# Strassen factors of the last layer's weights: made in every cell, or made once and streamed from HBM

## The chip, the cores and the metric

The kernel runs on one core of one Trainium2 chip. The metric is device time of one execution in microseconds (us). Three executions of the kernel before took 1265.14, 1265.29 and 1268.28 us; the median is 1265.29.

Engines are named as in the profile: PE is TensorE's matmul, PEld its weight load, DVE is VectorE, ACT is ScalarE, POOL is GpSimd, SP is SyncE, which issues all DMAs here.

## The reference, cut to what matters

Three stages follow each other: attention with 32 packed queries (8 batches, 8 heads, 576 tokens, width 64), an expert layer with softmax gating and layer norm (512 to 1024 to 512), and a maxout layer ("moe2", 512 to 768 to 512), on 4608 tokens. The change touches the last stage, and the decoding of its weights:

```
def _moe2_ref(x, w1, w2, w3, w_out):
    h = np.maximum(np.maximum(x @ w1, x @ w2), x @ w3)
    return (h @ w_out).astype(np.float32)
```

The weights arrive as 64-bit floats. The kernel reads them as pairs of 32-bit words and turns them into 32-bit floats itself ("decoding").

## The kernel before, in words

**Precision.** PE multiplies in a reduced 32-bit format. Every operand is split into a high part (an ACT copy into that format) and a low part (the value minus the high part), and a product is three matmuls: high x high, high x low, low x high.

**First half (to about 549 us).** A loop over 36 tiles of 128 tokens does attention for one batch after another (class Packed), the hidden layer (tok_hidden, L494), the transposes (L559) and the output product y (L574), which goes to a DRAM tensor, ydram. Letters in CFG['s1'] say in which order these steps are issued. At each letter D the pieces loaded at the D before are decoded and up to CFG['dr'] new ones loaded: 128 rows by 256 columns each, one ACT step, five DVE steps (L127 to L136), one POOL step (L141). The decoded moe2 weights go to the DRAM tensors wdram and wodram. Only the first EARLY x 128 = 512 of the 768 columns of w1, w2, w3, and the first 512 of the 768 rows of w_out, are done here.

**Second half.** x is cut into six passes (p) of 768 tokens, each a 2x2 block of 384-token columns and halves of the 512 inputs. The 768 hidden units are three column pairs (c) of 2 x 128, and there are three weight matrices (x, printed as w1 to w3). One "cell" (p, c, x), 54 in all, computes a 2x2 block product of one weight block and the x block by Strassen's scheme in Winograd's form: seven products instead of eight, each 2 row blocks x 3 matmuls of 384 columns, 42 matmuls per cell (L701). The four PSUM banks ba, bb, bc and bd hold products; a later product is added into a bank that has been used (start=False) after the bank's first content was read:

```
product(bc, 's3', 't3'); v_ = bc + u      (DVE, L734)
product(bd, 's1', 't1'); result(1, 1, bd, v_)
product(ba, 'a12', 'b21', start=False)
product(bc, 'a22', 't4', start=False)     (must wait until v_ was read from bc)
```

The token factors (b11, t1 to t4, b21, b22) are made once per pass: load_y (L654), four differences on DVE (sums_y, L660), seven splits on ACT with DVE and POOL in turn (splits_y, L674). The weight factors are made anew **for every cell**, one cell ahead, by split_w (L634): four sums s1 to s4 on DVE (L638 to L641, tile s, one buffer), three high parts on ACT (L647), three low parts on POOL (L648: al of 512, sl of 1024, cl of 256 columns; two buffers each). All raw weights stay in SBUF. The columns beyond 512 are decoded in the first pass (decode_late, L605).

After the first cell of a pass, after its fourth and at its end come output blocks: per 128 hidden units out_step (L914) does 9 matmuls of 512 columns (L918), after split_hidden (L747) made the high and low part of h (ACT L750, POOL L751). store (L923) scales on ACT and writes out. Per pass these are 108 matmuls (54 in the first pass and 54 more at the very end).

**Order.** The program is traced in this order, and a scheduler of the language gives each engine a fixed sequence at compile time, by readiness in its own model, earlier traced first. On the chip each engine runs its sequence in order; a waiting instruction holds all behind it. SP's DMAs are such a sequence too.

Of the kernel before, what the change touches and what calls it, by code (L numbers as in the profile page):

```python
# [18 lines left out]
def f32(ap):  # L19
# [17 lines left out]
    dr=2,  # L37
# [7 lines left out]
    early=4,  # L45
    wr=3,
    l3='v',
    mx3='v',
# [7 lines left out]
    d3='g',  # L56
# [6 lines left out]
def kernel(  # L63
# [20 lines left out]
    EARLY = CFG['early']  # L84
# [18 lines left out]
    wodram = tc.dram_tile([DF2, DM], F32, name="wodram")  # L103
    ydram = tc.dram_tile([P, KDM, NT], F32, name="ydram")
# [494 lines left out]
    wr = [[None] * 3 for _ in range(KF2)]  # L599
    w2h = [None] * KF2  # L600
    w2l = [None] * KF2
    raw_b, split_b, split_a = {}, {}, {}
    B_ORDER = ('b11', 't2', 't3', 't1', 'b21', 't4', 'b22')

    def decode_late(dst, src):  # L605
        raw = raw_p.tile([P, KDM, P, 2], I32, tag="raw", name="raw")
        nc.sync.dma_start(out=raw, in_=src)
        t = raw_p.tile([P, DM], F32, tag="dt", name="dt")
        decode(dst, raw.rearrange("r k f t -> r (k f) t"), t, None, ENG[CFG['mx3']], ENG[CFG['d3']])()

    def load_w2(c, x, pool):
        wr[c][x] = pool.tile([P, KDM, P], F32, name=f"wr{c}_{x}")
        if c < EARLY:
            nc.sync.dma_start(
                out=wr[c][x], in_=wdram[x, :, c * P:(c + 1) * P].rearrange("(k r) f -> r k f", r=P)
            )
        else:
            decode_late(
                wr[c][x].rearrange("r k f -> r (k f)"),
                words((w1, w2, w3)[x])[:, c * P:(c + 1) * P, :].rearrange("(k r) f t -> r k f t", r=P),  # L620
            )

    def load_wo2(c, pool):
        wt = wst.tile([P, DM], F32, tag="wt", name="wt3")
        if c < EARLY:
            nc.sync.dma_start(out=wt, in_=wodram[c * P:(c + 1) * P, :])
        else:
            decode_late(wt, words(w_out2)[c * P:(c + 1) * P, :, :].rearrange("r (k f) t -> r k f t", f=P))
# [5 lines left out]
    def split_w(c, x):  # L634

        a, a2 = wr[2 * c][x], wr[2 * c + 1][x]
        s = st_p.tile([P, 4, 2, P], F32, tag="s", name="s")
        nc.vector.tensor_tensor(out=s[:, 0], in0=a2[:, :2, :], in1=a2[:, 2:, :], op=ALU.add)  # L638
        nc.vector.tensor_tensor(out=s[:, 1], in0=s[:, 0], in1=a[:, :2, :], op=ALU.subtract)
        nc.vector.tensor_tensor(out=s[:, 2], in0=a[:, :2, :], in1=a2[:, :2, :], op=ALU.subtract)  # L640
        nc.vector.tensor_tensor(out=s[:, 3], in0=a[:, 2:, :], in1=s[:, 1], op=ALU.subtract)  # L641
        ah, al = (sw_p.tile([P, 2, 2, P], F32R, tag=n, name=n) for n in ("ah", "al"))
        ch, cl = (sw_p.tile([P, 2, P], F32R, tag=n, name=n) for n in ("ch", "cl"))
        sh, sl = (sw_p.tile([P, 4, 2, P], F32R, tag=n, name=n) for n in ("sh", "sl"))
        av = a.rearrange("r (h k) f -> r h k f", h=2)
        for hi, lo, src in ((ah, al, av), (sh, sl, s), (ch, cl, a2[:, 2:, :])):
            nc.scalar.copy(hi, src)  # L647
            nc.gpsimd.tensor_tensor(out=lo, in0=src, in1=f32(hi), op=ALU.subtract)  # L648
        split_a[c, x] = dict(
            a11=(ah[:, 0], al[:, 0]), a12=(ah[:, 1], al[:, 1]), a22=(ch, cl),  # L650
            **{f's{i + 1}': (sh[:, i], sl[:, i]) for i in range(4)},
        )

    def load_y(p):  # L654
        for key, k, n in (('b11', 0, 0), ('b12', 0, 1), ('b22', 1, 1), ('b21', 1, 0)):
            t = raw_b[p, key] = yb_p.tile([P, 2, TW], F32, tag=key, name=key)
# [3 lines left out]
    def sums_y(p):  # L660

        def step(key, x, y, dst=None):
            def do():
                t = raw_b[p, dst] if dst else yb_p.tile([P, 2, TW], F32, tag=key, name=key)
                nc.vector.tensor_tensor(out=t, in0=raw_b[p, x], in1=raw_b[p, y], op=ALU.subtract)
                raw_b[p, key] = t
# [21 lines left out]
    def cell(p, c, x):  # L688


        fa = split_a.pop((c, x))
# [39 lines left out]
        add(out=u, in0=bb, in1=q, op=ALU.add)  # L731
        product(bc, 's3', 't3')
        v_ = row("v")
        add(out=v_, in0=bc, in1=u, op=ALU.add)  # L734
        product(bd, 's1', 't1')
        result(1, 1, bd, v_)
        product(ba, 'a12', 'b21', start=False)
        if x == 0:
            nc.scalar.copy(cur[0, 0], ba)
        else:  # L740
            add(out=cur[0, 0], in0=ba, in1=cur[0, 0], op=ALU.max)
        product(bc, 'a22', 't4', start=False)
        result(1, 0, bc, u)
        product(bd, 's4', 'b22', start=False)
        result(0, 1, bd, u)

# [136 lines left out]
    yb_p = ctx.enter_context(tc.tile_pool(name="yb", bufs=1, **right))  # L883
    w0_p = ctx.enter_context(tc.tile_pool(name="w0", bufs=1, **right))
    st_p = ctx.enter_context(tc.tile_pool(name="st", bufs=1, **right))
    sw_p = ctx.enter_context(tc.tile_pool(name="sw", bufs=2, **right))
    sy_p = ctx.enter_context(tc.tile_pool(name="sy", bufs=1, **right))
    load_y(0)
    for x in range(3):
        for c in range(2):  # L890
            load_w2(c, x, w0_p)
    before = [*sums_y(0), *splits_y(0), lambda: split_w(0, 0)]
    j = NB - 1
    for _ in range(2 * KFF):
        step_y(j, 2 * KFF)
        step_t(j, done[j] + CFG['look'])
        if before:
            before.pop(0)()
    late.close()


    wpool = ctx.enter_context(tc.tile_pool(name="w2", bufs=1, reuse_waits="tile"))
    wst = ctx.enter_context(tc.tile_pool(name="wst", bufs=1, reuse_waits="tile"))
    raw_p = ctx.enter_context(tc.tile_pool(name="raw", bufs=1, reuse_waits="tile"))
    z_p = ctx.enter_context(tc.tile_pool(name="scales", bufs=1, reuse_waits="tile"))
    cur_p = ctx.enter_context(tc.tile_pool(name="cur", bufs=2, reuse_waits="tile"))
    keep_p = ctx.enter_context(tc.tile_pool(name="kept", bufs=8, reuse_waits="tile"))
    tmp_p = ctx.enter_context(tc.tile_pool(name="tmp", bufs=2, reuse_waits="tile"))
    h_p = ctx.enter_context(tc.tile_pool(name="h2", bufs=3, reuse_waits="tile"))
    o_p = ctx.enter_context(tc.tile_pool(name="o", bufs=3, reuse_waits="tile"))  # L910
# [22 lines left out]
    todo = [lambda c=c: load_wo2(c, wpool) for c in range(2)]  # L933
    for x in range(3):
        todo += [lambda c=c, x=x: load_w2(c, x, wpool) for c in (2, 3)]
    for x in range(3):
        todo += [lambda c=c, x=x: load_w2(c, x, wpool) for c in (4, 5)]
    todo += [lambda c=c: load_wo2(c, wpool) for c in range(2, KF2)]
    cells = [(p, c, x) for p in range(NT // TW // 2) for c in range(KF2 // 2) for x in range(3)]
    z = scales()  # L940
    kept, first_half, ops = [], [], None
    for n, (p, c, x) in enumerate(cells):
        for _ in range(3):
            if todo:
                todo.pop(0)()
        if n + 1 < len(cells):
# [63 lines left out]
```

## Time and profile before

| | before |
|---|---|
| median of three runs | 1265.29 us |
| profiled execution | 1260.86 us |
| its span, first to last instruction | 1258.8 us |
| mean granted TensorE clock | 0.946 of full speed |
| busy: PE, PEld, DVE, ACT, POOL | 89%, 73%, 70%, 42%, 40% |
| HBM read, written | 63.97 MB, 23.07 MB |

The profile is one execution, taken by the hardware profiler. A group row reads: line, engine, operation, tile written <- tiles read, shape, count | busy us, mean ns of one | idle time of the engine just before, and what ended it. "L648" is a line of the kernel. Matmul ends are modelled: two consecutive ones overlap in the record, so their rate is read from their starts.

### The profile page before, as it was taken

The numbers are of one execution on the slowest core, as the hardware profiler recorded it, in microseconds if no ns is written. First come the engines' busy times: TensorE is split into PE (matmuls) and PEld (weight loads), VectorE is DVE, ScalarE is ACT, GpSimd is POOL, SyncE is SP. The second block draws the span as 40 slices with busy tenths as digits, with TensorE's granted clock in tenths as the row PEclk, the third lists the DMA queues.
The fourth block names the chain that finished last, engine by engine and source line by source line (L and its number), as shares of the span: only waits on it lengthen the run. The fifth ranks groups of instructions, "written<-read, shape, count | busy, mean of one in ns | idle before, by whom it ended". The sixth has DMA issues, their size and how long they took to land.

```text
span 1258.8 us, 17413 instructions
## 1 busy us (share of the span) xinstructions
PE 1115.5 (89%) x6308; PEld 918.6 (73%) x6308; DVE 884.8 (70%) x1668; ACT 528.2 (42%) x1025; POOL 505.4 (40%) x385
## 2 busy tenths in 40 slices
PE   4789899999999999798778998888888879879888
PEld 3357576777677778577666887788878868878887
DVE  6798777787878776779899558555845584564561
ACT  4476464655555544523243323322422333233222
POOL 5442210111111100247467546455734564465552
PEclk8799999999999999898998998898899889989999
DMA  8734344444444400533112001100200020001001
GB/s 235 171 90 117 102 115 128 121 132 115 137 116 125 111 18 17 161 97 94 51 42 68 26 1 38 39 25 1 76 26 1 1 76 26 1 1 51 1 1 50
DMA packets 96550, 88.16 MB, mean 70 GB/s; under 512 B 47569, under 2 KB 79313, under 8 KB 96465
## 3 DMA queue, kind: packets, MB, share of 16 engines
q1 hardware_dynamic: 96464, 87.06, 24.3%
q8 instruction: 49, 0.80, 0.3%
q14 instruction: 37, 0.30, 0.1%
HBM read 63.97 MB, written 23.07 MB: 69 GB/s over the span
## 4 chain that ended last, share of the span: by engine, by line
PE 51%; DVE 16%; issue 8%; POOL 7%; ACT 4%; DMA 3%; ACTq 0%; POOLq 0%; DVEq 0%
PE m L701 21%; PE o L918 10%; PE y L582 8%; PE h L507 5%; POOL sl L648 4%; PE tp L564 2%; PE mp L402 1%; DVE u L731 1%; DVE v L734 1%; DVE s L640 1%; DMA wdram<-dt 1%; DVE raw L131 1%; POOL hl L751 1%; DVE r L723 1%; DVE dt L127 1%
## 5 line engine op out<-in xcount | busy, mean ns | idle before, releaser
L648 POOL TENSOR_TENSOR sl<-s,sh 128x1024 fp32r<-128x1024 f32 x54 | 135.6, 2511 | 51.1 <-ACT sh L647 46.6
L638 DVE TENSOR_TENSOR s<-wr 128x256 f32<-128x256 f32 x54 | 50.1, 927 | 116.1 <-POOL sl L648 115.1
L648 POOL TENSOR_TENSOR al<-wr,ah 128x512 fp32r<-128x512 f32 x54 | 76.7, 1421 | 133.6 <-ACT ah L647 133.5
L582 PE MATMUL y<-lh,woh 128*128 128x512 f32 x288 | 119.4, 417 | 0.7 <-DVE yt L250 0.6
L582 PE MATMUL y<-ll,woh 128*128 128x512 f32 x288 | 115.3, 401 | 1.6 <-DVE ll L571 1.6
L582 PE MATMUL y<-lh,wol 128*128 128x512 f32 x288 | 115.0, 399 | 1.1 <-POOL wol L219 1.1
L141 POOL TENSOR_TENSOR dt<-raw,dt 128x256 f32<-128x256 f32 x40 | 32.7, 817 | 205.1 <-DVE dt L136 105.3
L701 PE MATMUL m<-t4h,ch 128*128 128x384 f32 x108 | 45.4, 420 | 75.5 <-DVE v L734 75.5
L647 ACT CAST ah<-wr 128x512 fp32r<-128x512 f32 x54 | 33.5, 620 | 147.9 <-PE m L701 141.6
L918 PE MATMUL o<-w2l,hh 128*128 128x512 f32 x216 | 87.7, 406 | 5.4 <-POOL w2l L632 5.4
L918 PE MATMUL o<-w2h,hh 128*128 128x512 f32 x216 | 88.0, 407 | 0.0
L701 PEld LDWEIGHTS m<-t4h,ch 128*128 128x128 f32 x108 | 23.2, 215 | 88.0 <-DVE v L734 88.0
L918 PE MATMUL o<-w2h,hl 128*128 128x512 f32 x216 | 87.1, 403 | 0.0
L647 ACT CAST sh<-s 128x1024 fp32r<-128x1024 f32 x54 | 56.7, 1050 | 49.8 <-PE m L701 24.0
L648 POOL TENSOR_TENSOR cl<-wr,ch 128x256 fp32r<-128x256 f32 x54 | 51.1, 946 | 54.9 <-ACT ch L647 54.9
L731 DVE TENSOR_TENSOR u<-m,q 128x384 f32<-128x384 f32 x54 | 29.7, 550 | 53.7 <-PE m L701 52.6
L582 PEld LDWEIGHTS y<-lh,woh 128*128 128x128 f32 x288 | 54.5, 190 | 15.3 <-DVE yt L250 1.0
L582 PEld LDWEIGHTS y<-lh,wol 128*128 128x128 f32 x288 | 54.6, 190 | 14.2 <-POOL wol L219 1.6
L570 ACT ACTIVATE lh<-tp,g_sb 128x512 fp32r<-128x512 f32 x72 | 47.3, 686 | 41.2 <-PE tp L564 41.2
L582 PEld LDWEIGHTS y<-ll,woh 128*128 128x128 f32 x288 | 54.7, 190 | 12.9 <-DVE ll L571 2.3
L724 DVE TENSOR_TENSOR kept<-r,kept 128x384 f32<-128x384 f32 x72 | 58.1, 807 | 1.8
L513 DVE TENSOR_REDUCE nm<-h 128x1 f32<-128x1024 f32 x36 | 43.9, 1218 | 20.2 <-PE h L507 19.9
(196 smaller groups left out, 3386.6 us busy)
## 6 DMA issues: line engine op xcount, KB each, us to landing
kt<-in_k_dram SPq DMA_DIRECT2D x16, 576.0 KB, 5.0
vt<-in_v_dram SPq DMA_DIRECT2D x16, 576.0 KB, 5.0
ydram<-yt SPq DMA_DIRECT2D x36, 256.0 KB, 3.2
b<-ydram SPq DMA_DIRECT2D x24, 384.0 KB, 3.4
out_dram<-ob SPq DMA_DIRECT2D x36, 256.0 KB, 2.0
qtl<-in_q_dram SPq DMA_DIRECT2D x64, 128.0 KB, 3.2
raw<-in_moe_w_dram SPq DMA_DIRECT2D x24, 256.0 KB, 2.8
raw<-in_moe_w_in_dram SPq DMA_DIRECT2D x8, 512.0 KB, 8.5
```

The costliest lines, as they stand in the source:

```text
L141: add.tensor_tensor(out=dst, in0=f32(hi), in1=t, op=ALU.add)
L507: nc.tensor.matmul(h[:, n, :], lhsT=x, rhs=m[:, g, n * 512:(n + 1) * 512], start=(i == 0), stop=(i == len(ops) - 1),)
L513: nc.vector.tensor_reduce(out=nm, in_=hv, axis=AX.X, op=ALU.max, negate=True)
L570: nc.scalar.activation(lh, tp, AF.Copy, scale=gc)
L582: nc.tensor.matmul(ys[half][m], lhsT=w[:, kc, ms], rhs=x, start=(kc == 0 and i == 0), stop=(kc == KFF - 1 and i == 2),)
L638: nc.vector.tensor_tensor(out=s[:, 0], in0=a2[:, :2, :], in1=a2[:, 2:, :], op=ALU.add)
L647: nc.scalar.copy(hi, src)
L648: nc.gpsimd.tensor_tensor(out=lo, in0=src, in1=f32(hi), op=ALU.subtract)
L701: nc.tensor.matmul(out, lhsT=w, rhs=y, start=start and i == 0, stop=i == len(ops) - 1, skip_group_check=not start,)
L724: add(out=cur[m, n], in0=r, in1=cur[m, n], op=ALU.max)
L731: add(out=u, in0=bb, in1=q, op=ALU.add)
L918: nc.tensor.matmul(ops[i], lhsT=x[:, ts], rhs=w, start=(c == 0 and n == 0), stop=(c == KF2 - 1 and n == 2),)
```

## The change

Weight factors are made once, in the first pass, for each of the nine weight blocks (c, x). a11, a12 and a22 (high and low) stay in SBUF. s1 to s4 (high and low together, 256 KB each) are written to a DRAM tensor, sdram, and from the second pass on are read back, four tiles per cell, through a ring of nine buffers, issued at the start of the cell before. In the first pass the split of the next cell is cut into steps, and cell() calls one step after each of its products; so are load_wo2 and, in the last cell of a pass, the token splits, which were issued after the cell. The differences and the load of the next pass's tokens move to later cells of the pass. All moe2 weights are decoded in the first half: 56 pieces of 256 columns instead of 40, three per turn instead of two; decode_late is gone. The buffers of h and of the output go from three to two each, and several pools change sides.

```
-    dr=2,
+    dr=3,
-    early=4,
+    sdram = tc.dram_tile([DF2 // 2 // P * 3, 4, P, 4 * P], F32, name="sdram")
+    def split_w(c, x, pool):
+        raw = []
+        def load():
+            for m in range(2):
+                t = w_p.tile([P, 2, 2, P], F32, tag="w", name="wt2")
...
+                nc.sync.dma_start(out=..., in_=wdram[x, :, cs].rearrange("(k r) f -> r k f", r=P))
+        def part(hi, lo, src):
+            nc.scalar.copy(hi, src)
+            nc.gpsimd.tensor_tensor(out=lo, in0=src, in1=f32(hi), op=ALU.subtract)
+        def plus(key, x, y, op):
+            t = sums_w[key] = w_p.tile([P, 2, P], F32, tag=key, name=key, bufs=1)
+            nc.vector.tensor_tensor(out=t, in0=x, in1=y, op=op)
+        def piece(key):
+            t = sr_p.tile([P, 2, 2, P], F32R, tag="s", name=key)
+            part(t[:, 0], t[:, 1], sums_w[key])
+            nc.sync.dma_start(out=sdram[3 * c + x, S_ORDER.index(key)], in_=...)
+            split_s[c, x, key] = t
+        def first():    # ah, al kept in SBUF; sums s1, s2
+        def second():   # piece s2; sum s3
+        def third():    # piece s3; sum s4
+        def fourth():   # piece s1
+        def fifth():    # ch, cl kept in SBUF; piece s4
+        return [load, first, second, third, fourth, fifth]
+    def load_s(c, x):
+        for i, key in enumerate(S_ORDER):
+            t = split_s[c, x, key] = sr_p.tile([P, 2, 2, P], F32R, tag="s", name=key)
+            nc.sync.dma_start(out=f32(t).rearrange("r n k f -> r (n k f)"), in_=sdram[3 * c + x, i])
...
-    def cell(p, c, x):
+    def cell(c, x, between):
+        def others():
+            if between:
+                between.pop(0)()
         product(ba, 'a11', 'b11')
         q = row("q")
         nc.scalar.copy(q, ba)
+        others()
         product(bb, 's2', 't2')
...
+    sr_p = ctx.enter_context(tc.tile_pool(name="sr", bufs=9, **right))
+    w_p = ctx.enter_context(tc.tile_pool(name="w", bufs=3, **right))
-    h_p = ctx.enter_context(tc.tile_pool(name="h2", bufs=3, reuse_waits="tile"))
-    o_p = ctx.enter_context(tc.tile_pool(name="o", bufs=3, reuse_waits="tile"))
+    h_p = ctx.enter_context(tc.tile_pool(name="h2", bufs=2, reuse_waits="tile"))
+    o_p = ctx.enter_context(tc.tile_pool(name="o", bufs=2, reuse_waits="tile"))
+    for n in range(NC - 1):
+        chores[n] = prep[n][1:]
+        if n + 1 < len(prep):
+            chores[n].append(prep[n + 1][0])
+        if n < KF2:
+            chores[n].append(lambda c=n: load_wo2(c, wpool))
+    for p in range(1, NP2):
+        chores.setdefault(NC * p - 7, []).append(lambda p=p: load_y(p))
+        for i, f in enumerate((0, 1, 2, 3)):
+            chores.setdefault(NC * p - 5 + i, []).append(lambda p=p, i=i: fresh(p)[i]())
+        chores.setdefault(NC * p - 1, []).extend([lambda: None] + splits_y(p))
     for n, (p, c, x) in enumerate(cells):
-        if n + 1 < len(cells):
-            split_w(*cells[n + 1][1:])
+        if p and n + 1 < len(cells) or n == NC - 1:
+            load_s(*cells[n + 1][1:])
-        cell(p, c, x)
+        cell(c, x, chores.pop(n, []))
```

## Rows read from the trace of the kernel before

**Rows 1.** The page, part 1: busy us (share of the span) xinstructions.
```profile
PE 1115.5 (89%) x6308; PEld 918.6 (73%) x6308; DVE 884.8 (70%) x1668; ACT 528.2 (42%) x1025; POOL 505.4 (40%) x385
```

**Rows 2.** Stretches of the first half: length, busy (x) by engine, clock, DMA share, GB/s.
```profile
210.00:240.00 30.00, 29.84 (x170) 21.17 (x167) 28.23 (x64) 16.79 (x37) 5.76 (x7) 1.00 0.32 89
300.00:330.00 30.00, 29.77 (x209) 23.35 (x209) 21.52 (x54) 17.33 (x41) 3.27 (x5) 1.00 0.57 159
```

**Rows 3.** Stretches: the first pass, and the five later ones.
```profile
548.80:680.30 131.50, 104.77 (x481) 91.47 (x481) 116.06 (x175) 42.33 (x73) 78.15 (x52) 0.92 0.23 69
680.30:1258.80 578.50, 507.12 (x2485) 465.16 (x2483) 340.61 (x549) 188.39 (x316) 306.18 (x206) 0.94 0.07 25
```

**Rows 4.** The same stretches, PE and PEld of one line: L701, L918, L582.
```profile
680.30:1258.80 578.50, 367.87 (x1890) 350.51 (x1889) 0.94 0.07 25
...
680.30:1258.80 578.50, 144.42 (x595) 114.83 (x594) 0.94 0.07 25
...
548.80:680.30 131.50, 11.94 (x49) 8.84 (x48) 0.92 0.23 69
```

**Rows 5.** One undisturbed cell (L701) and one output block (L918).
```profile
1192.40:1199.70 7.30, 7.29 (x42) 7.29 (x42) 1.00 0.01 2
...
1149.10:1161.70 12.60, 12.57 (x54) 9.97 (x54) 1.00 0.00 0
```

**Rows 6.** Waits from 690 us on: us in total, times, longest.
```profile
DVE s L638 <- POOL sl L648: 107.5, 41, 3.7
...
PE m L701 <- DVE v L734: 65.5, 29, 5.4
```

**Rows 7.** Timeline of DVE in a stalled cell: start, us, instruction [idle before].
```profile
1182.52 1.20 DVE L638 TENSOR_TENSOR s<-wr 128x256 f32<-128x256 f32 x1 [2.99 <-POOL sl L648]
1183.65 0.55 DVE L731 TENSOR_TENSOR u<-m,q 128x384 f32<-128x384 f32 x1
...
1185.39 0.55 DVE L734 TENSOR_TENSOR v<-m,u 128x384 f32<-128x384 f32 x1
```

**Rows 8.** Timeline of PE in a twin of that cell, two passes earlier.
```profile
958.64 0.46 PE L701 MATMUL m<-t4h,ch 128*128 128x384 f32 x1 [3.25 <-DVE v L734]
...
959.86 0.52 PE L701 MATMUL m<-t4l,ch 128*128 128x384 f32 x1
960.18 0.52 PE L701 MATMUL m<-t4h,cl 128*128 128x384 f32 x1
```

**Rows 9.** Stretch just behind that wait.
```profile
959.50:961.00 1.50, 1.50 (x6) 1.50 (x6) 0.26 (x1) 0.40 (x1) 0.05 (x1) 0.50 0.04 11
```

**Rows 10.** Groups by line, whole span.
```profile
L648 POOL TENSOR_TENSOR sl<-s,sh 128x1024 fp32r<-128x1024 f32 x54 | 135.6, 2511 | 51.1 <-ACT sh L647 46.6 <-PE m L701 2.7 <-DMA raw<-in_moe_w_dram 1.6
...
L648 POOL TENSOR_TENSOR al<-wr,ah 128x512 fp32r<-128x512 f32 x54 | 76.7, 1421 | 133.6 <-ACT ah L647 133.5
...
L648 POOL TENSOR_TENSOR cl<-wr,ch 128x256 fp32r<-128x256 f32 x54 | 51.1, 946 | 54.9 <-ACT ch L647 54.9
...
L751 POOL TENSOR_TENSOR hl<-kept,hh 128x384 fp32r<-128x384 f32 x36 | 39.3, 1099 | 15.2 <-ACT hh L750 15.2
...
L750 ACT CAST hh<-kept 128x384 fp32r<-128x384 f32 x36 | 18.3, 512 | 34.1 <-PE o L918 34.1
```

**Rows 11.** Groups of DVE by line, 161.6 to 424.8 us.
```profile
L131 DVE SCALAR_TENSOR_TENSOR raw<-raw,dt 128x256 int32<-128x256 int32 x31 | 14.3, 460 | 0.6
```

**Rows 12.** DMA issues: count, KB each, median us from issue to landing.
```profile
wr<-wdram SPq DMA_DIRECT2D x12, 256.0 KB, 4.8
...
wt<-wodram SPq DMA_DIRECT2D x4, 256.0 KB, 3.2
```

**Rows 13.** Instructions of line L724: ns min/median/max, first and last start.
```profile
L724 DVE TENSOR_TENSOR kept<-r,kept x72: 542/560/2209, 578.5 to 1234.7; 128x384 f32<-128x384 f32 x72
```

**Rows 14.** Timeline of PE in the hand-over.
```profile
529.92 1.11 PE L564 MATMUL tp<-ident,u 128*128 128x128 f32 x4 [6.84 <-DVE u L531]
```

**Rows 15.** Stretch of the hand-over between the halves.
```profile
516.20:531.00 14.80, 7.96 (x40) 6.21 (x38) 12.74 (x16) 8.30 (x12) 5.26 (x3) 0.81 0.88 273
```

More of the change, by code (lines that the diff above doesn't have):

```diff
@@ L590, in y_product @@
                 nc.sync.dma_start(out=ydram[:, half * KDM // 2 + m, j * TB:(j + 1) * TB], in_=yt)
-    wr = [[None] * 3 for _ in range(KF2)]
+    NC = KF2 // 2 * 3
     w2h = [None] * KF2
     w2l = [None] * KF2
-    raw_b, split_b, split_a = {}, {}, {}
+    raw_b, split_b, split_a, split_s = {}, {}, {}, {}
     B_ORDER = ('b11', 't2', 't3', 't1', 'b21', 't4', 'b22')
[L605 to L621, printed above, removed]
-    def load_wo2(c, pool):
[L624 to L628, printed above, removed]
+    S_ORDER = ('s2', 's3', 's1', 's4')
+    def load_wo2(c, pool):
+        wt = w_p.tile([P, DM], F32, tag="w", name="wt3")
+        nc.sync.dma_start(out=wt, in_=wodram[c * P:(c + 1) * P, :])
         w2h[c] = pool.tile([P, DM], F32R, name=f"w2h{c}")
@@ L632, in load_wo2 @@
         nc.gpsimd.tensor_tensor(out=w2l[c], in0=wt, in1=f32(w2h[c]), op=ALU.subtract)
[L634 to L646, printed above, removed]
+    def split_w(c, x, pool):
[3 more added lines that the diff above has]
+                t = w_p.tile([P, 2, 2, P], F32, tag="w", name="wt2")
+                cs = slice((2 * c + m) * P, (2 * c + m + 1) * P)
+                nc.sync.dma_start(
+                    out=t.rearrange("r h k f -> r (h k) f"),
+                    in_=wdram[x, :, cs].rearrange("(k r) f -> r k f", r=P),
+                )
+                raw.append(t)
+        def part(hi, lo, src):
@@ new lines, in piece @@
+        def piece(key):
+            t = sr_p.tile([P, 2, 2, P], F32R, tag="s", name=key)
+            part(t[:, 0], t[:, 1], sums_w[key])
+            nc.sync.dma_start(out=sdram[3 * c + x, S_ORDER.index(key)], in_=f32(t).rearrange("r n k f -> r (n k f)"))
+            split_s[c, x, key] = t
+        def first():
+            ah, al = (pool.tile([P, 2, 2, P], F32R, name=f"{n}{c}_{x}") for n in ("ah", "al"))
+            part(ah, al, raw[0])
+            split_a[c, x] = dict(a11=(ah[:, 0], al[:, 0]), a12=(ah[:, 1], al[:, 1]))
+            plus('s1', raw[1][:, 0], raw[1][:, 1], ALU.add)
+            plus('s2', sums_w['s1'], raw[0][:, 0], ALU.subtract)
@@ new lines, in second @@
+        def second():
+            piece('s2')
+            plus('s3', raw[0][:, 0], raw[1][:, 0], ALU.subtract)
+        def third():
+            piece('s3')
+            plus('s4', raw[0][:, 1], sums_w['s2'], ALU.subtract)
+        def fourth():
+            piece('s1')
+        def fifth():
+            ch, cl = (pool.tile([P, 2, P], F32R, name=f"{n}{c}_{x}") for n in ("ch", "cl"))
+            part(ch, cl, raw[1][:, 1])
+            split_a[c, x]['a22'] = ch, cl
+            piece('s4')
+        return [load, first, second, third, fourth, fifth]
@@ L734, in cell @@
         add(out=v_, in0=bc, in1=u, op=ALU.add)
+        others()
         product(bd, 's1', 't1')
         result(1, 1, bd, v_)
+        others()
         product(ba, 'a12', 'b21', start=False)
@@ L931, in banks_o, with fresh @@
         return [ps_o.tile([P, DM], F32, tag="o", name="o") for _ in range(TW // P)]
[L933 to L939, printed above, removed]
+    NP2 = NT // TW // 2
+    cells = [(p, c, x) for p in range(NP2) for c in range(KF2 // 2) for x in range(3)]
+    chores = {}
+    prep = [split_w(*cells[n][1:], wpool if cells[n][1] else w0_p) for n in range(1, NC)]
+    prep[0][0]()
+    for n in range(NC - 1):
[9 more added lines that the diff above has]
+        chores.setdefault(NC * p - 1, []).extend([lambda: None] + splits_y(p))
+    sums_of = {}
+    def fresh(p):
+        if p not in sums_of:
+            sums_of[p] = sums_y(p)
+        return sums_of[p]
     z = scales()
```

60 lines of the change are left out of this document (24 added, 36 removed).

## The prediction

> **What bounds the kernel now.** I read the page first, then stretches, then waits. The page's totals give TensorE (PE) 89% busy [rows 1], but that is a mean over two halves. The stretches split it. In the attention and first-expert half, PE is within 1% of always busy even where VectorE (DVE) is at 28.2 of 30 us [rows 2]: PE bounds it. The second half is 54 cells of 42 matmuls: nine cells per pass, six passes. The first pass, from the first cell's first matmul, takes 131.5 us, the other five 578.5 us together [rows 3]; the matmuls by line are counted in [rows 4]. What would PE alone need? A cell that never waits shows it: 42 matmuls in 7.29 us, 0.1736 us each; an undisturbed output block of 54 takes 12.57 us, 0.2328 each [rows 5].
>
> Later passes: 1890 x 0.1736 + 594 x 0.2328 = 328.1 + 138.3 = 466.4 us, so 112 of the 578.5 are lost. First pass: 378 x 0.1736 + 54 x 0.2328, and 48 leftover matmuls of the half before, 11.2, make 89.4; 42 of 131.5 are lost.
>
> Who takes it, the waits say: in the later passes PE stood 65.5 us for v (L734), and DVE stood 107.5 us at L638 for POOL's sl [rows 6]. The DVE timeline of one stalled cell joins the two. L638, the first weight sum of the next cell, sits 2.99 us for POOL; u, ready long before, is queued behind it, then a second sum, and v starts at 1185.39 [rows 7]. PE's a22 product adds into the bank that v reads, so it cannot start: in a twin of this cell PE waits 3.25 us. Behind that wait the spacing is 0.32 us instead of 0.17 at a granted clock of 0.50, that is 1.2 of 2.4 GHz [rows 8, 9]. So 65.5 us of waiting, about 40 us at the low clock, and a few us of final store make the 112. POOL, though only 40% busy, decides: each cell redoes the same splits, sl 2.51, al 1.42 and cl 0.95 us [rows 10].
>
> **The change, part by part.** The terms are changes of the profiled span, 1258.8 us.
>
> *1. Five later passes.* 45 of the 54 split_w calls have no successor: 4 DVE sums, 3 ACT copies, 3 POOL subtractions each (4.88 us of POOL). In their place come four 256 KB loads per cell on SP. With no L638 ahead of u and v, v is a 0.55 us step on an engine with about 5 us of work in a 7.29 us cell. What is late next? The candidates: the four y splits on DVE in the last cell of a pass, which now stand between products ahead of u and v; the ring (a rival below); the hidden-state buffers, cut from 3 to 2. For these, a copy may start only when PE has finished the step two before, and 0.51 + 1.10 us of copy and subtract [rows 10] must fit in one step of nine matmuls, 2.10 us: it fits, with about 0.4 us to spare once POOL has nothing else. The output buffers, also 3 to 2, make ACT wait for a store of some 2 to 3 us before the third evacuation; q is queued behind it, but v has two products' time (2.1 us) of slack. I leave about 2 us per pass and 5 at the end, 15 us; the gain is 112 - 15 = 97. Bounds: nothing left but the end store (gain 106), or 45 us left (gain 67).
>
> *2. First pass.* Gone from it: late decoding of eight 512-column pieces, five DVE steps each; the longest, L131, takes 0.46 us for 256 columns [rows 11], so up to 8 x 5 x 0.92 = 37 us of DVE. Kept: the weight sums. Changed: POOL's sl of 1024 columns becomes four of 256, so that POOL has 1.42 + 5 x 0.95 = 6.2 us a cell, plus 1.4 (taken as al, same size) in the six cells that load an output-weight block: 7.6, against PE's 7.29. New on SP, in this order: two raw loads per cell, four stores of 256 KB that each wait for POOL, one output-weight load; the next cell's raw loads queue behind the stores if the scheduler keeps program order. So this pass is not freed, only lightened. Upper bound of its loss: 60, if a raw load of 4.8 us [rows 12] stands in series with POOL in each of eight cells (38 on top of the 22 below); lower: 5, if all overlaps. The nearest row is the later passes of today, with 4.88 us of POOL per cell and a loss of 112/5 = 22 us each. I take 22: gain 42 - 22 = 20 (bounds 37 and -18).
>
> A two-input VectorE operation between SBUF tiles has a spread: L724 takes 0.56 us at the median and up to 2.21 [rows 13]. The Trainium skill (SBUF — State Buffer, Who interferes with whom) says such an instruction and a GpSimd one that reads SBUF take one port pair in turn, the loser blocked for the whole instruction; the spread agrees. By that rule a first-pass cell needs the sum of both: 6.2 us of POOL and, where x is 1 or 2, seven such DVE steps (four sums, three maxima) at 0.56, 10.1 us; where x is 0 only the sums, 8.4. Five and three such cells exceed 7.29 by 17 us (an estimate), so the low end of this pass's loss would be 17, not 5, and the most it could give 25, not 37.
>
> *3. First half.* 16 more decode pieces (56 instead of 40), three per turn instead of two. Each has five DVE steps, none longer than L131's 0.46 us [rows 11]: at most 2.3 us, 37 us in all if none is hidden. Each also adds a load and a store on SP and 0.8 us of POOL. What hides it: DVE has 30 - 21.5 = 8.5 us free in a light stretch, but 1.8 in a heavy one [rows 2], and the extra is about 0.75 piece per 13 us tile, some 4 us per 30. Light stretches swallow it, heavy ones overflow by about 2 us, in some three or four places, partly absorbed by the transposes made ahead. I take +4, bounds 0 and +37.
>
> *4. Hand-over.* PE stands 6.84 us for the last L531, which stands behind the y sums on DVE [rows 14]. The y tiles move to a part of SBUF that other attention buffers held, probably free earlier, so some sums may run before the last tokens; and six weight loads beside the y loads [rows 15] shrink to two. I take -4 (bounds -9, +5).
>
> **Sum:** -97 - 20 + 4 - 4 = -117; span 1141.8. The profiled execution took 1260.86, 2.1 outside its span: 1143.9. The median shown, 1265.29, is 4.4 above that execution, so on its scale 1148.
>
> **The rivals.**
> *A, the front pays.* The first pass stays as slow as now (+20) and the extra decoding is not hidden (+33): 1201. For: DVE's 28.2 of 30 us in heavy stretches, POOL at 7.6 us against 7.29. Against: PE's gapless rows there today, and up to 37 us of DVE taken out of the first pass. 15%.
>
> *B, slower: the ring is late.* Place: SP's queue and the four loads between one cell's products and the next. A load of the same size lands in 3.2 us [rows 12]. Were they served one after the other, a cell's four need 12.8 us against 7.29. Three of nine cells have an output block to cover them, six do not: 5.5 x 6 x 5 = 165 us, 1313. It decides from 117/30 = 3.9 us per exposed cell, 11.2 us for four loads. Against: loads overlap; while the hand-over loads ran, 273 GB/s were moved [rows 15], at which a cell's 1.05 MB take 3.8 us. Also the ring holds nine tiles, so a whole next cell can be in flight. 6%.
>
> The Trainium skill (DMA: Bandwidth & Descriptors, Anatomy of one DMA) fits about 2.0 us plus the bytes at 436 GB/s to one transfer of GpSimd's queue, and advises 1 MiB ones; for 256 KB that is 2.6 us, and in series 10.4 per cell, an estimate of 1148 + 3.1 x 30 = 1241. The single landing above agrees in size; the 273 GB/s speaks against the series.
>
> *C, the change doesn't do what it says.* v stays late for another reason (DVE held by the y splits or POOL's port), so that the later passes gain next to nothing: 1148 + 97 = 1245. For: DVE runs instructions in a fixed order. Against: where POOL is done in time the cell is dense today [rows 5], with the same u, v and result steps. 6%.
>
> **How the numbers follow.** Forecast 68%, A 15%, B 6%, C 6%; 5% for better than all, with the later passes dense and the first pass at its low bound: 1148 - 9 - 17 - 4 = 1118. The likeliest is 1148. From 1120 to 1205 the range takes in A and nearly all of the forecast's bounds, and leaves out B, C and the best tail. A measurement here tells 0.3%, 4 us, from no change. Only B is slower: 6%; between them and the mild cases 2% for no change; faster 92%.
>
> **What would show it.** Right: in the later passes no cell without an output block over 8 us, PE's wait for v near zero, granted clock 0.99 or more, POOL under 25% busy there. Ring loads: PE never waiting on a DMA. First pass near 110 us, its waits on DVE and POOL. First half: PE still over 29 of 30 us. Wrong: PE waiting for s tiles from the DRAM copy (B); v late with POOL idle (C); the first cell starting over 15 us later than 548.8 (A).

## The result, and the profile after

The kernel after takes 1154.80 us (median of four, 1152.18 to 1156.96), the one before 1265.22 us (median of four beside it). The ratio is 0.913, with a 95% interval of 0.910 to 0.916. Forecast: 1148, from 1120 to 1205. The profiled execution took 1152.18 us, its span is 1150.4: 108.4 less than before, where the sum said 117.

The page of the kernel after, its busy line [rows 1 before] and its line for the loads of the ring (count, KB each, median us from issue to landing):

```profile
PE 1072.8 (93%) x6308; PEld 889.5 (77%) x6308; DVE 762.5 (66%) x1528; ACT 449.1 (39%) x925; POOL 297.9 (26%) x285
...
s<-sdram SPq DMA_DIRECT2D x180, 256.0 KB, 2.8
```

The same 6308 matmuls; POOL's time falls from 505 to 298 us. The span divides at three landmarks: the start of the last tile's layer-norm reduction (L513 before, L509 after), the first cell's first matmul, the second pass's first matmul. Stretches of the kernel before, from 161 us (length, then busy us of PE, PEld, DVE, ACT, POOL, clock, DMA share, GB/s):

```profile
161.00:516.20 355.20, 350.98 (x2321) 261.02 (x2320) 271.54 (x631) 189.50 (x406) 44.91 (x51) 1.00 0.37 101
516.20:548.80 32.60, 24.06 (x104) 18.79 (x103) 28.11 (x34) 16.61 (x26) 15.31 (x8) 0.79 0.59 185
```

and of the kernel after, the last two answering to [rows 3]:

```profile
161.00:536.50 375.50, 356.44 (x2330) 261.72 (x2329) 296.84 (x719) 196.82 (x422) 56.30 (x67) 1.00 0.42 118
536.50:559.70 23.20, 19.76 (x94) 15.51 (x92) 16.61 (x22) 16.05 (x28) 12.25 (x9) 0.93 0.15 53
559.70:673.00 113.30, 98.25 (x481) 89.09 (x480) 80.69 (x131) 38.91 (x83) 65.56 (x65) 0.94 0.58 184
673.00:1150.40 477.40, 470.53 (x2485) 440.89 (x2483) 238.90 (x376) 105.93 (x188) 102.88 (x78) 1.00 0.41 124
```

| stretch | before | after | difference | forecast |
|---|---|---|---|---|
| first half | 355.2 | 375.5 | +20.3 | +4 |
| hand-over | 32.6 | 23.2 | -9.4 | -4 |
| first pass | 131.5 | 113.3 | -18.2 | -20 |
| later passes | 578.5 | 477.4 | -101.1 | -97 |

The border between hand-over and first pass is not sharp: 48 leftover matmuls of the half before lie in the first cell in both kernels, but they are spread out longer now and end 18.0 us behind that cell's first matmul, 12.5 before. Counted to the last of them (561.3 and 577.7 us), the hand-over gives 3.9 us and the first pass 23.7.

In the later passes all that PE waits for (us in total, times, longest) is one line; [rows 6] had 65.5 us for v:

```profile
PE m L722 <- DVE r L744: 1.6, 4, 0.4
```

The cell that answers to the stalled one of [rows 7], on DVE: nothing stands ahead of u and v, and v starts 0.97 us after u, not 1.74.

```profile
1089.60 0.56 DVE L757 TENSOR_TENSOR u<-m,q 128x384 f32<-128x384 f32 x1 [5.74 <-PE m L722]
1090.57 0.56 DVE L761 TENSOR_TENSOR v<-m,u 128x384 f32<-128x384 f32 x1 [0.41 <-PE m L722]
```

In the first half the two stretches of [rows 2] show where time was lost. The heavy one changed little; the light one, where cover was assumed, lost 2.1 us of PE's work:

```profile
210.00:240.00 30.00, 29.59 (x171) 21.41 (x167) 27.03 (x67) 17.25 (x39) 6.30 (x8) 1.00 0.30 83
300.00:330.00 30.00, 27.63 (x196) 21.25 (x195) 19.82 (x54) 16.87 (x40) 2.98 (x4) 1.00 0.53 153
```

### The profile page after: what moved, and what is told of

Same layout as the page of the kernel before. It is cut to its first block, busy times and chain, and to the rows that moved or that the text cites. A ratio compares the mean times of both kernels' runs of the same rounds, so it can differ in the third digit from the quotient of the medians.

```text
span 1150.4 us, 17592 instructions
## 1 busy us (share of the span) xinstructions
PE 1072.8 (93%) x6308; PEld 889.5 (77%) x6308; DVE 762.5 (66%) x1528; ACT 449.1 (39%) x925; POOL 297.9 (26%) x285
## 3 DMA queue, kind: packets, MB, share of 16 engines
HBM read 113.25 MB, written 34.60 MB: 129 GB/s over the span
## 4 chain that ended last, share of the span: by engine, by line
PE 45%; issue 4%; DVE 3%; POOL 1%; DMA 1%; ACT 0%; DVEq 0%; POOLq 0%; ACTq 0%
PE m L722 30%; PE o L951 13%; PE y L578 1%; DMA wt<-wdram 1%; DVE r L744 1%; DVE s L633 0%; DVE v L761 0%; DVE u L757 0%; POOL t4l L699 0%; POOL t1l L699 0%; POOL s L627 0%; DVE kept L745 0%; DMA out_dram<-ob 0%; POOL al L627 0%; POOL dt L137 0%
## 5 line engine op out<-in xcount | busy, mean ns | idle before, releaser
L137 POOL TENSOR_TENSOR dt<-raw,dt 128x256 f32<-128x256 f32 x56 | 45.2, 807 | 294.3 <-DVE dt L132 201.2
L784 POOL TENSOR_TENSOR hl<-cur,hh 128x384 fp32r<-128x384 f32 x36 | 41.9, 1163 | 242.9 <-ACT hh L783 242.9
L753 ACT COPY q<-m 128x384 f32<-128x384 f32 x54 | 25.9, 479 | 167.6 <-PE m L722 167.6
L951 PE MATMUL o<-w2l,hh 128*128 128x512 f32 x216 | 85.2, 395 | 0.0
L722 PE MATMUL m<-b22h,s 128*128 128x384 f32 x216 | 65.3, 343 | 2.8 <-DVE r L744 2.8
L578 PEld LDWEIGHTS y<-ll,woh 128*128 128x128 f32 x288 | 55.2, 192 | 14.5 <-DVE ll L567 4.1
L722 PE MATMUL m<-t2h,s 128*128 128x384 f32 x216 | 64.2, 337 | 0.0
L722 PE MATMUL m<-t1h,s 128*128 128x384 f32 x216 | 63.6, 334 | 0.0
L722 PE MATMUL m<-t3h,s 128*128 128x384 f32 x216 | 63.5, 334 | 0.0
L784 POOL TENSOR_TENSOR hl<-kept,hh 128x384 fp32r<-128x384 f32 x36 | 42.2, 1173 | 67.4 <-ACT hh L783 67.4
L509 DVE TENSOR_REDUCE nm<-h 128x1 f32<-128x1024 f32 x36 | 43.8, 1217 | 17.0 <-PE h L503 16.8
L567 DVE SCALAR_TENSOR_TENSOR ll<-tp,g_sb,lh 128x512 fp32r<-128x512 f32 x72 | 52.5, 741 | 3.2 <-ACT lh L566 3.1
L511 ACT ACTIVATE u<-h,nm 128x1024 f32<-128x1024 f32 x36 | 40.1, 1115 | 35.6 <-DVE nm L509 35.3
```

Source lines behind the costliest of these rows:

```text
L137: add.tensor_tensor(out=dst, in0=f32(hi), in1=t, op=ALU.add)
L509: nc.vector.tensor_reduce(out=nm, in_=hv, axis=AX.X, op=ALU.max, negate=True)
L511: nc.scalar.activation(u, hv, AF.Exp, bias=nm, accum_out=sums[:, t:t + 1])
L567: nc.vector.scalar_tensor_tensor(out=ll, in0=tp, scalar=gc, in1=f32(lh), op0=ALU.mult, op1=ALU.subtract)
L578: nc.tensor.matmul(ys[half][m], lhsT=w[:, kc, ms], rhs=x, start=(kc == 0 and i == 0), stop=(kc == KFF - 1 and i == 2),)
L722: nc.tensor.matmul(out, lhsT=w, rhs=y, start=start and i == 0, stop=i == len(ops) - 1, skip_group_check=not start,)
```

## The experiments

Twelve kernels ran, each against the kernel before on the same chip. "First half", "first pass" and so on are the stretches of the table above.

### The decoding moved, alone

```
-    dr=2,          # the kernel before
+    dr=3,
-    early=4,
+    early=6,
```

> The kernel before with only its decoding moved: all 56 pieces in the first half, three per turn, no late decoding; weight factors still made in every cell. Theory F (the extra decoding costs the first half, whatever the second half does): first tile-35 reduce at about 536 us instead of 516, first cell near 560; the first pass loses its late decoding, 131 to about 105-115 us; later passes unchanged at 578 us; time about 1255 to 1270. Rival (the later start comes from the new second half's buffers, not from decoding): first half as before, 516, and time near 1245.

1267.36 us, ratio 1.005 (1.003 to 1.007). Its stretches:

```profile
160.60:530.30 369.70, 354.07 (x2323) 260.30 (x2322) 292.54 (x712) 196.44 (x422) 55.19 (x67) 1.00 0.40 113
530.30:562.20 31.90, 22.93 (x101) 17.79 (x99) 29.74 (x39) 16.80 (x26) 14.79 (x9) 0.84 0.58 177
562.20:676.30 114.10, 95.66 (x481) 87.21 (x480) 75.94 (x130) 36.20 (x62) 65.15 (x43) 0.96 0.22 63
676.30:1263.80 587.50, 510.71 (x2485) 468.29 (x2483) 341.37 (x549) 189.47 (x319) 307.26 (x207) 0.93 0.07 25
```

The first half loses 14.5 us and the first pass wins 17.4, without any of the streaming. So moving the decoding makes most of the first half's loss, can make nearly the whole of the first pass's gain, and is worth nothing by itself. The later passes keep their loss, and take 9 us more than in the kernel before (587.5), where Theory F had them unchanged; no run here says why.

### How many pieces, and how they are dealt

Three variants of the kernel after. `pieces40` decodes only 40 pieces, two per turn; `even2` always two per turn; `late2` deals as the kernel before did up to tile 27 (two, at every fourth tile one) and two from tile 28 on.

```
-    dr=3,                                              # pieces40
+    dr=2,
...                                                   # blocks not decoded: read from decoded ones
-        for r0 in range(0, rows, P):
-            todo += [(w, dst, r0, f) for f in range(0, DF2 if w is not w_out2 else DM, DC)]
+        for r0 in range(0, rows if w is not w_out2 else 4 * P, P):
+            todo += [(w, dst, r0, f) for f in range(0, 4 * P if w is not w_out2 else DM, DC)]
...
-    for _ in range(2 if todo2 else CFG['dr'] if t % 4 else 1):
+    for _ in range(2):                                 # even2
+    for _ in range(2 if todo2 or t % 4 or t >= 28 else 1):  # late2
```

> The changed kernel with 40 pieces instead of 56, two per turn as before: the last 256 columns of w1 to w3 and the last 256 rows of w_out are not decoded, and their blocks are read from decoded ones, so the output is not the reference's; all instructions of the second half stay. Theory F: the first half goes back to its old length, first cell near 540-549, time about 1133 to 1140. Rival (the second half's buffers delay the first half or the hand-over): time stays above 1148.

> The changed kernel with two pieces at every turn instead of three at three turns of four and one at the fourth. Theory F1 (the cost is DVE's added time meeting full stretches): spreading evenly helps a little, the first half 3 to 8 us shorter, time 1147 to 1152. Rival F2 (the third piece of a turn itself holds ACT or SP, with two raw buffers and one dt buffer): nearly the whole 20 us come back, time 1135 to 1140.

> The changed kernel with the 56 pieces dealt as before up to tile 27 (two per turn, one at every fourth) and two per turn from tile 28 on, where no attention is left and DVE has 3 to 5 us free per tile. Theory F1 (an added decode step costs only where DVE's stretch is full): tile 35 at 517 to 522 us, time 1134 to 1139. Rival F3 (each piece costs its 1.3 us wherever it stands): tile 35 at 527 as with the even deal, time 1143 to 1146.

| | before | after | even2 | late2 | pieces40 |
|---|---|---|---|---|---|
| median, us | | 1154.80 | 1144.31 | 1137.10 | 1133.26 |
| ratio | | 0.913 | 0.907 | 0.900 | 0.898 |
| its 95% interval | | 0.910-0.916 | 0.904-0.910 | 0.898-0.902 | 0.895-0.900 |
| tile 8 to tile 28: us, pieces | 275.7, 32 | 288.7, 37 | 280.1, 38 | 275.6, 33 | 275.0, 32 |
| tile 28 to last reduction: us, pieces | 78.9, 0 | 86.9, 11 | 87.0, 10 | 85.2, 12 | 79.5, 0 |

(A tile's time here is the start of its layer-norm reduction; pieces are counted by their L127 steps, L131 before.) With 40 pieces the whole half takes 354.4 us, as before: the 16 pieces cost the kernel after 21.1 us. But they need not. Up to tile 28 the kernel after decodes five pieces more than the kernel before and pays 13.0 us, 2.6 each; two per turn, six more cost 4.4, 0.7 each; from tile 28 on, 10 to 12 pieces cost 6.3 to 8.1, again 0.5 to 0.8 each. So the size of a turn counts more than the number of pieces: three of them are up to 3 x 1.83 us of DVE, by the five steps of the kernel after (DVE by line, 160.9 to 536.5 us; busy, mean ns):

```profile
L127 DVE SCALAR_TENSOR_TENSOR raw<-raw,dt 128x256 int32<-128x256 int32 x48 | 22.3, 464 | 0.8
L132 DVE SCALAR_TENSOR_TENSOR dt<-raw,dt 128x256 f32<-128x256 uint32 x48 | 20.6, 429 | 0.4
L130 DVE TENSOR_SCALAR dt<-raw 128x256 int32<-128x256 int32 x48 | 15.2, 318 | 0.6
L123 DVE TENSOR_SCALAR dt<-dt 128x256 f32<-128x256 f32 x48 | 15.0, 313 | 28.2 <-ACT dt L118 27.8
L124 DVE TENSOR_SCALAR dt<-dt 128x256 int32<-128x256 int32 x48 | 14.6, 305 | 0.5
```

All that PE waits for between tile 8 and tile 28 comes to 13.7 us in the kernel after, 3.6 in the kernel before and 3.2 in late2. The largest part is for ACT, which copies pTz, a transposed tile of the attention, out of PSUM; the kernel after, then late2:

```profile
PE tp L322 <- ACT pTz L244: 6.0, 7, 1.5
```

```profile
PE tp L322 <- ACT pTz L244: 1.6, 2, 1.3
```

Two of the three longest of those seven waits stand behind a decode step of ACT that waits for the store of an earlier piece, because the tile dt has one buffer. This is ACT 2.0 us before PE's wait that ends at 440.97:

```profile
438.91 0.43 ACT L118 ACTIVATE dt<-raw 128x256 f32<-128x256 f32 x1 [1.98 <-DMA wdram<-dt]
```

So it is shown that bursts cost more. Whether they do so through DVE's time (Theory F1) or through ACT behind that buffer (as in rival F2) is not separated: late2 falls where F1 put it, even2's 1144.31 lies between the ranges of both, and pieces40 where Theory F put it.

late2 is the fastest version that computes the whole, 17.7 us under the kernel after. Three of its pieces fall into the hand-over, which takes 27.7 us there against 23.2.

### One decode step moved to POOL

```
-    mx2='v',       # late2
+    mx2='g',
```

> As late2, and the first of the five DVE steps of each piece (the maximum, 0.31 to 0.36 us) is done by GpSimd, which is under 15% busy in the first half. If DVE's time is what the first half pays for: 1 to 5 us shorter than late2. Rival (GpSimd's step takes DVE's port or is slow, and delays the chain of the piece): as late2 or longer.

1152.78 us, ratio 0.913 (0.910 to 0.916), 15.7 slower than late2: a miss for the version that counts DVE's time alone. The first half to the last reduction ends at 536.5 us, against 520.9. The step's rows, here and in late2 (160 to 530 us):

```profile
L123 POOL TENSOR_SCALAR dt<-dt 128x256 f32<-128x256 f32 x43 | 40.0, 931 | 113.5 <-ACT dt L118 112.5 <-DMA qtl<-in_q_dram 1.1
```

```profile
L123 DVE TENSOR_SCALAR dt<-dt 128x256 f32<-128x256 f32 x46 | 14.7, 320 | 19.8 <-ACT dt L118 19.5
```

The step takes 931 ns on POOL instead of 320, and the next DVE step of the piece waits for it in order: 27.0 us in 27 waits (DVE L124 for POOL L123) from tile 8 on. From there the step makes 6.7 of the 15.6 us by which the last reduction comes later. The other 8.9 stand already at tile 8 (169.0 against 160.1 us), where the granted clock of the two profiles differs too (0.81 against 0.89 in the first 62 us); what makes them is open.

### No steps between the products

```
         def others():
-            if between:
-                between.pop(0)()
+            return
...
         while between:          # at the cell's end
-            others()
+            between.pop(0)()
```

> The changed kernel with the other steps issued after a cell's seven products and none between them. Theory R (the gain is the streaming of s1 to s4; the scheduler moves the steps anyway): later passes 478 us as they are, the first pass 113 to 125; time 1155 to 1166. Rival I (the steps between the products carry the gain): the splits of the next pass delay cell 8 and the first pass goes back to 131 us or more; time above 1185.

1154.25 us, ratio 0.913 (0.911 to 0.916); first pass 113.5, later passes 477.3. Where the steps are traced changes nothing, because the language's scheduler places them anyway: in the two traces PE, DVE and ACT run the same steps in the same order from the first cell on. For the same reason rival I is not tested: the steps still stand between the products on the chip.

### A shorter ring, and more raw loads ahead

```
-    sr_p = ctx.enter_context(tc.tile_pool(name="sr", bufs=9, **right))
+    sr_p = ctx.enter_context(tc.tile_pool(name="sr", bufs=5, **right))   # ring5; late2_w5r7: 7
...
-    w_p = ctx.enter_context(tc.tile_pool(name="w", bufs=3, **right))
+    w_p = ctx.enter_context(tc.tile_pool(name="w", bufs=5, **right))     # late2_w5r7, on late2
```

> The changed kernel with five ring buffers instead of nine: one tile ahead instead of a whole cell. A tile then loads only when the product four places before it has been done. Theory L (loads overlap, land in 2.8 us and four tiles' products last over 4 us): later passes within 5 us of 477, time 1155 to 1165. Rival B (the ring is near its limit): s2 of each cell, asked for only late in the cell before, arrives late; 1 us or more per cell, time above 1200.

> late2 with five raw weight buffers instead of three, paid for with two ring buffers (nine to seven, which five already showed to be enough later on). If the first pass waits for raw loads (ACT stood 16.5 us for them there): first pass 109 to 98-104 us, time 1126 to 1133. Rival (POOL and DVE in turn set the first pass, 17 us over dense by the two-input estimate): first pass 107 us or more, time 1134 to 1139.

ring5: 1153.57 us, ratio 0.913 (0.910 to 0.916); later passes 477.3. Five buffers, one more than a cell needs, hide the loads as nine do in the later passes, so rival B was far from deciding. late2_w5r7: 1140.86 us, ratio 0.903 (0.899 to 0.907), no gain over late2; its first pass takes 110.6 against 109.2, where 98 to 104 was expected. So two more raw buffers buy nothing there. The ring, which the first pass fills too, was shortened with them; ring5's first pass is only 1.6 us longer than the kernel after's (114.9 against 113.3), too little to hide the 5 to 11 us expected.

### The low part of the sums left out

```
-        sh, sl = (sw_p.tile([P, 4, 2, P], F32R, tag=n, name=n) for n in ("sh", "sl"))   # the kernel before
+        sh = sl = sw_p.tile([P, 4, 2, P], F32R, tag="sh", name="sh")
...
+            if hi is not sh:
                 nc.gpsimd.tensor_tensor(out=lo, in0=src, in1=f32(hi), op=ALU.subtract)
```

> The kernel before without POOL's low part of the four weight sums (sl, 2.5 us per cell): the high part stands in for it in the products, so the output is not the reference's; DVE's sums, ACT's copies, al and cl stay, redone in every cell. Theory Q (what PE waits for is sl's turn on POOL, through L638 at the head of DVE): PE's wait for v falls under 15 us, later passes from 578 to 475-500 us, time 1150 to 1185, as much as streaming gave. Rival W (the two-deep buffers of the factors, whose copies wait for PE, keep the chain slow): later passes stay above 530 us, time above 1210.

1153.77 us, ratio 0.912 (0.909 to 0.915). The later passes:

```profile
658.30:1152.70 494.40, 476.17 (x2485) 439.39 (x2483) 323.41 (x551) 189.15 (x317) 202.36 (x164) 1.00 0.09 30
```

and what PE waits for from 690 us on:

```profile
PE m L702 <- DVE v L735: 5.7, 3, 1.9
```

Without POOL's 54 sl the later passes fall from 578.5 to 494.4, and PE's wait for v goes from 65.5 to 5.7 us, though every cell still makes its sums, high parts, al and cl. So 84 of the 101 us hang on this one subtraction. The first pass, too, takes 113.8 us instead of 131.5, with the late decoding still in it:

```profile
544.50:658.30 113.80, 98.58 (x481) 86.36 (x480) 103.48 (x173) 41.16 (x71) 56.10 (x42) 0.97 0.25 77
```

### A second buffer for the sums

In the kernel before; `sums2` gives the pool two buffers, `sums_turn` two tiles strictly in turn; both give h2 two instead of three, for room.

```
-    st_p = ctx.enter_context(tc.tile_pool(name="st", bufs=1, **right))
+    st_p = ctx.enter_context(tc.tile_pool(name="st", bufs=2, **right))      # sums2
...
-        s = st_p.tile([P, 4, 2, P], F32, tag="s", name="s")
+        turn[0] ^= 1
+        s = st_p.tile([P, 4, 2, P], F32, tag=f"s{turn[0]}", name="s")       # sums_turn
```

> The kernel before with two buffers for the weight sums s instead of one (and two instead of three for h, to make room). Theory Q (PE's waits come from L638 standing at the head of DVE's sequence for POOL's sl, because s has one buffer): with a second buffer L638 rarely waits, v is on time, later passes fall from 578 to about 480-500 us, time about 1160 to 1185, so most of the gain without any streaming. Rival W (it is the amount of POOL and DVE work per cell, 4.88 us of POOL with the port taken in turn): DVE's wait moves to another place, later passes stay above 545, time above 1230.

> As sums2, but the two buffers of the weight sums are used strictly in turn (two names, one buffer each), whereas a pool of two may hand back the buffer that was just released; in sums2 L638 still started 34 ns after the end of the previous cell's sl, every time. Theory Q (the wait on sl comes through the buffer of s): L638 no longer starts at sl's end, PE's wait for v falls under 20 us, later passes under 510 us, time under 1190. Rival P (L638 cannot run beside sl whatever its buffer, since both read SBUF in turn; or another wait takes its place): later passes above 540 us, time above 1225.

sums2: 1248.67 us, ratio 0.989 (0.987 to 0.991); sums_turn: 1248.07, ratio 0.989 (0.984 to 0.993). Later passes 560.0 and 560.3. So Theory Q missed in both, and the figures are those of its rivals. The second buffer saves 18 us, and DVE waits for sl still (sums_turn from 690 us on):

```profile
DVE s L641 <- POOL sl L651: 89.5, 33, 3.0
```

Each time it waited for sl, the first sum starts 0.03 to 0.04 us after an end of sl. From sums_turn's timelines, DVE and POOL:

```profile
1162.18 0.42 DVE L641 TENSOR_TENSOR s<-wr 128x256 f32<-128x256 f32 x1 [2.29 <-POOL sl L651]
1171.92 1.21 DVE L641 TENSOR_TENSOR s<-wr 128x256 f32<-128x256 f32 x1 [2.99 <-POOL sl L651]
1181.27 0.43 DVE L641 TENSOR_TENSOR s<-wr 128x256 f32<-128x256 f32 x1 [2.89 <-POOL sl L651]
1192.88 0.43 DVE L641 TENSOR_TENSOR s<-wr 128x256 f32<-128x256 f32 x1 [2.29 <-POOL sl L651]
```

```profile
1159.64 2.50 POOL L651 TENSOR_TENSOR sl<-s,sh 128x1024 fp32r<-128x1024 f32 x1 [0.20 <-ACT sh L650]
1169.48 2.40 POOL L651 TENSOR_TENSOR sl<-s,sh 128x1024 fp32r<-128x1024 f32 x1
1178.83 2.41 POOL L651 TENSOR_TENSOR sl<-s,sh 128x1024 fp32r<-128x1024 f32 x1 [0.94 <-ACT sh L650]
1190.33 2.52 POOL L651 TENSOR_TENSOR sl<-s,sh 128x1024 fp32r<-128x1024 f32 x1 [0.19 <-PE m L704]
1200.19 2.39 POOL L651 TENSOR_TENSOR sl<-s,sh 128x1024 fp32r<-128x1024 f32 x1
1205.96 2.41 POOL L651 TENSOR_TENSOR sl<-s,sh 128x1024 fp32r<-128x1024 f32 x1 [0.46 <-PE m L704]
```

Which sl is it? Both lists run to the end of the 54 splits. The sum at 1162.18 is the fourth from the end, split 51; the sl that releases it is the sixth from the end, split 49. Two splits back: that is the one that frees a buffer of two. The compiled sequence agrees: in the kernel before, the sum of split k stands ahead of v of cell k-2 and waits for sl of split k-1; with two buffers it stands ahead of v of cell k-3 and waits for sl of split k-2. The scheduler used the buffer to move the sum a cell forward, and it met POOL there as before. In sums2, too, the sum waits for the sl of two splits back, not for the previous cell's. The wait is for the buffer, then, not for a shared port, which I had taken for the likelier reading after sums2. Where a sum starts beside a POOL subtraction, the trace shows it as a longer step and not as idle time before it: at 1001.63 us one takes 2.08 us beside POOL's t2l instead of 0.41.

### The sums held behind v

So I kept the sums behind v, by a false dependence: two columns of v are copied into s first, and overwritten by the sums.

```
     def split_w(c, x):                  # the kernel before
         s = st_p.tile([P, 4, 2, P], F32, tag="s", name="s")
+        if newest:
+            nc.vector.tensor_copy(s[:, ::2, 0, 0], newest["v"][:, :2])
...
         add(out=v_, in0=bc, in1=u, op=ALU.add)
+        newest["v"] = v_
```

> The kernel before, all sums and splits kept in every cell, with one step added: before its first sum, split_w copies two columns of v of the newest traced cell into the sum tile s (both values are overwritten by the sums), so that the compiled sequence of DVE must hold the sums behind v instead of ahead of u and v. One 128x2 copy per cell more, nothing less. Theory O (order and semaphore: in the kernel before, the first sum of split k stands in DVE's sequence ahead of u and v of the cell two before k and waits there until sl of split k-1 is done with the one buffer of s): DVE's wait for sl disappears from the top of the waits or is paid where v is already out, PE's wait for v falls from 65 to under 10 us, the five later passes take 490 to 505 us instead of 578, total 1165 to 1195, about as without sl. Theory S (the sums beside POOL, by whatever path, cost DVE the same time wherever they stand, or the sums now come too late for the next cell's factors): PE waits for v or for the next cell's factors instead, later passes 550 or more, total 1235 or more.

1233.72 us, ratio 0.976 (0.972 to 0.980); later passes 556.2. The mechanism of theory O came true, its price did not; theory S has the later passes, and misses its total by 1.3 us. PE's three largest waits from 700 us on:

```profile
PE m L704 <- DVE kept L723: 25.1, 13, 2.3
PE m L704 <- DVE cur L745: 10.1, 10, 1.0
PE m L704 <- DVE v L737: 5.2, 7, 0.9
```

The wait for v is nearly gone (65.5 us before), and others have taken its place: the results. The timeline of DVE shows how:

```profile
1156.06 0.56 DVE L737 TENSOR_TENSOR v<-m,u 128x384 f32<-128x384 f32 x1
1157.51 0.96 DVE L640 COPY s<-v 128x2 f32<-128x2 f32 x1 [0.89 <-POOL sl L651]
1158.51 1.44 DVE L641 TENSOR_TENSOR s<-wr 128x256 f32<-128x256 f32 x1
1159.87 0.55 DVE L723 TENSOR_TENSOR kept<-m,v 128x384 f32<-128x384 f32 x1
```

The first result, kept, starts 3.8 us after v, behind a copy that waits for sl and a sum that takes 1.44 us (0.42 alone) while POOL subtracts. PE waits 2.29 us for it, and the clock drops again (0.83 from 1155 to 1165 us). So the placing of the sums is worth about 22 us; the rest up to no_sl's 84 needs sl gone. How much of that rest is the buffer's loop (sums, sh, sl, sums) and how much the longer DVE steps beside POOL, no run here separates.

## Why the prediction was right, and where it was off

**Later passes, -97 forecast, -101.1 measured.** The reading was right: sl on POOL, a sum of the next cell ahead of u and v, PE behind v. no_sl shows the first link; sums_turn and v_first show that the waiting sum was the form of the loss, not all of it: with the sums merely moved behind v the prediction's "with no L638 ahead of u and v" gave 22 us, and without sl it was 84. The last 17 came with the rest of the change (no al, cl, sums and copies in the later passes), which no run takes apart. Of the 15 us left over, 11 were left (477.4 - 466.4), 5.3 of them behind the last matmul: cells without an output block take 7.3 to 7.4 us, the clock is 1.00, POOL is 22% busy (102.9 / 477.4). What I set aside for the y splits and the smaller buffers was hardly needed: PE waits 1.6 us.

**First pass, -20 forecast, -18.2 measured.** Without the late decoding alone the pass gains 17.4 us (early6), without sl alone 17.7 (no_sl). So the two gains don't add, and no run says which of them the kernel after owes its 18.2 to. The loss is 113.3 - 89.4 = 23.9 us against 22 taken. That it came so near is in part luck: the 22 were read from passes in which POOL's sl of 1024 columns decides, and here PE waits 15.0 us, of which 9.9 are for v, 3.9 for the copy of an output of the half before and 1.2 for results, at a granted clock of 0.94. The waits for v look like the old stall on a small scale; DVE and POOL of the kernel after, in a first-pass cell:

```profile
626.52 0.56 DVE L757 TENSOR_TENSOR u<-m,q 128x384 f32<-128x384 f32 x1 [4.77 <-PE m L722]
628.27 1.47 DVE L633 TENSOR_TENSOR s<-wt,wt 128x256 f32<-128x256 f32 x1 [1.19 <-POOL s L627]
629.66 0.54 DVE L761 TENSOR_TENSOR v<-m,u 128x384 f32<-128x384 f32 x1
```

```profile
627.51 0.73 POOL L627 TENSOR_TENSOR s<-s,s 128x256 fp32r<-128x256 f32 x1
628.20 1.26 POOL L608 TENSOR_TENSOR w2l<-wt,w2h 128x512 fp32r<-128x512 f32 x1
```

A sum ahead of v waits 1.19 us for POOL, then takes 1.47 us where 0.41 is its time alone; it ends 0.28 us after POOL's w2l. PE waits 2.40 us for this v, and 9.9 us for v in the whole pass.

The Trainium skill (SBUF — State Buffer, Who interferes with whom) says that a VectorE instruction with two SBUF inputs contends with a GpSimd one that reads SBUF, for a pair of ports that is locked and not shared out. This row agrees: the sum starts 0.07 us after w2l and ends 0.28 us after it. The prediction's estimate by that rule, at least 17 us of loss, lies under the 23.9 measured. It took 6.2 us of POOL for a cell's splits where 5.2 are measured (590.1 to 599.4 us); with 5.2 the same sum makes about 10. The runs cannot part this from the waits for buffers.

**First half, +4 forecast, +20.3 measured.** This is the term that was mis-sized, by 16 us; the other terms gave back 8 of them. The step that failed: "Light stretches swallow it, heavy ones overflow by about 2 us". The number of pieces was right and so was the time of one (1.83 us, at most 2.3 said); but I spread them evenly, 0.75 per tile, where three come at once, among steps of ACT and DVE that PE waits for. The light stretch above lost 2.1 us, and the sign "PE still over 29 of 30 us" failed there (27.63). Dealt in twos the decoding costs 6.2 us there (late2: 275.6 + 85.2 from tile 8 to the last reduction, before 275.7 + 78.9), close to the +4, with 45 pieces in it and not 48.

**Hand-over, -4 forecast, -9.4 or -3.9 measured,** by which border is taken. PE's wait for the last tile's u, 6.84 us before [rows 14], is 2.6 now. That this comes from the y tiles' new place is not tested; it does not come from the decoding, since early6's hand-over takes 31.9 us.

**The rivals.** A was half right: much of its first half came (+20.3 of at most +37), its first pass did not. B: the loads land in 2.8 us, PE waits for none of them, and five buffers do. The Trainium skill (DMA: Bandwidth & Descriptors, Anatomy of one DMA) gives about 2.0 us plus the bytes at 436 GB/s for one transfer of GpSimd's queue, which is 2.6 us, an estimate, for a load; the loads here, on SP's queue, took 2.8. Served in series they would have made 1241 by that estimate, which the 1154.80 excludes. C fell: in the later passes PE never waits for v.

## What to carry to other kernels

Ask of a waiting instruction both who stands behind it and what it is waiting for: moving it (v_first) or giving it another buffer (sums2) mostly moved the wait, while taking away the work it waited for gained about four times as much. Work that was made once and streamed back cost PE no wait here, since its loads (2.8 us) fit beside the products. And filler on engines that the bound engine depends on was priced by the size of its bursts here: three pieces per turn cost 2.6 us each, two per turn 0.5 to 0.8.

## What was not expected of the hardware

A maximum with a constant over 128x256 floats takes 931 ns on POOL and 320 on DVE, on average. A copy of 128x2 (v_first, L640) took 0.17 us on DVE alone and 0.96 beside a subtraction of POOL (hl, from 1157.44 us). HBM reads rose from 63.97 to 113.25 MB, with no wait of PE for them in the later passes.
